# Down projection by seven float32 block products on one core, with block sums on GpSimd and 251-column chunks

## The chip, the cores and the metric

The kernel runs on one core of a Trainium2 chip. Five engines work side by side, each through its own queue in order: TensorE (PE; its weight loads are shown apart as PEld), VectorE (DVE), ScalarE (ACT), GpSimd (POOL) and SyncE (SP), which here only issues DMAs. They wait for each other by semaphores. The metric is the device time of one execution in microseconds (us); three executions of the kernel before have a median of 2159.93 us.

## The reference

```python
x: (8, 3008, 256) float32      w_in: (256, 2048)      w_out: (2048, 256)
X = fft(fft(x, axis=1), axis=2).real        # Fourier mixing of sequence and features
h = X.reshape(24064, 256) @ w_in
g = maximum(0.01 * h, h)                    # leaky ReLU
out = g @ w_out                             # (24064, 256)
```

Everything is in float32, the products on TensorE too.

## The kernel before

**Folding.** The feature transform of width 256 is multiplied into `w_in` once, at the start: `wf` holds the cosine and the sine part (256 rows of 2048 hidden units, two blocks of 128), `wn` the one feature that is its own mirror image. What is left is the sequence transform. The host lays out the rows of x so that a row and its mirror images lie in one tile; `fold_x` (L168) adds and subtracts them, so that a transform needs 3 products of 128 rows for an even and 3 for an odd part.

**Units and blocks.** A unit is one batch b and one parity c of the output frequencies, 16 units in all. `dft` (L276) makes one of a unit's two `mix` tiles (cosine block, sine block): 6 products of 377 or 376 columns into two PSUM tiles, then `butterfly` (L270) copies the even part on ScalarE and makes a plus and a minus half on VectorE. Each half is a block: 32 blocks of 377 or 376 columns. `spread` (L302) fetches the unit's row for the feature that `wn` serves, broadcast to all partitions (`nb`).

**A step** is one block j and one slice f of 128 hidden units: 512 steps.
- `up` (L315): two products of the block's columns, `cos_ps` and `sin_ps` (L320); on VectorE `cos = nb * wn + cos_ps` (L322), then `cos + sin_ps` and `cos - sin_ps` (L325, L326), which are the hidden values of two output columns that mirror each other; on ScalarE the leaky ReLU in place (L327). The result is `g`, five buffers in turn.
- `down` (L330): four products (L337), two column halves of g by two halves of the 256 outputs, added up over the 16 slices in four PSUM banks (`sum_ps`). After the last slice ScalarE copies the four banks (L343) and SP issues two DMAs to the output (L344).

`sum_ps` has four banks, `cos_ps`, `sin_ps` and `dft_ps` share the other four. `down` runs two steps behind `up` (`lag`, L356). The loop (L357) puts `spread`, `fold_x` and `dft` of the next unit beside certain steps, and the load of the next batch's x. The program's scheduler then sets the order on each queue, so that work can stand earlier than the loop says: with two buffers for x the load and the fold of batch 1 stand in the start, among the conversions of the weights (L223 to L229, seven VectorE operations for each 128 x 512 piece, through `raw` tiles of their own, three buffers).

Of the kernel before, what the change touches and what calls it, by code (L numbers as in the profile page):

```python
# [30 lines left out]
F32 = mybir.dt.float32  # L33
I32 = mybir.dt.int32
U32 = mybir.dt.uint32
ALU = mybir.AluOpType
# [5 lines left out]
NI = 3  # L42

KW = [377, 376]
KC = 377
NF = F // P
WN = 512
SLOPE = 0.01
# [60 lines left out]
def chunks():  # L109


    out, at = [], 0
    for b in range(B):
        for c in range(2):
            for sg in range(2):
                out.append((b, c, sg, at, KW[c]))
                at += 2 * KW[c]
    return out, at


def columns():

    at = np.zeros(B * S, np.int64)
    for b, c, sg, first, n in chunks()[0]:
        k = 2 * np.arange(n) + c
        plus, minus = (k, (S - k) % S) if sg == 0 else ((H + k) % S, H - k)
        at[b * S + minus] = first + n + np.arange(n)
        at[b * S + plus] = first + np.arange(n)
    return at
# [3 lines left out]
def tile_fnet_leaky_relu(  # L133
# [55 lines left out]
    wn = const.tile([P, NF], F32, name="wn")  # L189
    wo = const.tile([P, NF, D], F32, name="wo")  # L190
    nyx = const.tile([P, 2, 2, NI, 2, B], F32, name="nyx")
# [59 lines left out]

    def w_out_part(f):
        nf = WN // D
        raw = load_w(w_out[f * P : (f + nf) * P, :].rearrange("(c p) d -> p c d", p=P))
        to_f32(wo[:, f : f + nf, :].rearrange("p c d -> p (c d)"), raw, w_out.dtype)

# [12 lines left out]

    def butterfly(plus, minus, even_ps, odd_ps, m, kw):  # L270
        ev = work.tile([P, KC], F32, tag="ev", bufs=2, name="ev")
        nc.scalar.copy(ev[0:m, 0:kw], even_ps[0:m, 0:kw])  # L272
        nc.vector.tensor_tensor(plus, ev[0:m, 0:kw], odd_ps[0:m, 0:kw], op=ALU.add)  # L273
        nc.vector.tensor_tensor(minus, ev[0:m, 0:kw], odd_ps[0:m, 0:kw], op=ALU.subtract)  # L274

    def dft(u, blk):  # L276

        b, c = u
        z, kw = zs[b], KW[c]
        t = work.tile([P, 2, KC], F32, tag=f"mix{blk}", bufs=2, name=f"mix{blk}")  # L280
# [3 lines left out]
        butterfly(t[:, 0, 0:kw], t[:, 1, 0:kw], pe, po, P, kw)  # L284
        mixed.setdefault(u, {})[blk] = t
# [5 lines left out]
    nc.vector.tensor_tensor(nya[:, 1], nyb[:, 0], nyb[:, 1], op=ALU.subtract)  # L291
    nyq_dram = dram.tile([B, 2, 2, KC], F32, name="nyq_dram")

    def nyquist(c):
        pe, po = dft_ps(), dft_ps()
        for r, pt in ((0, pe), (1, po)):
            sequence(pt, B, lambda i: nya[:, c, i, r, :], r, c)
        t = work.tile([P, 2, KC], F32, tag="mix0", bufs=2, name="nyq")
        butterfly(t[0:B, 0, 0 : KW[c]], t[0:B, 1, 0 : KW[c]], pe, po, B, KW[c])
        nc.sync.dma_start(nyq_dram[:, c, :, 0 : KW[c]], t[0:B, :, 0 : KW[c]])  # L300

    def spread(u):  # L302

        b, c = u
        t = work.tile([P, 2, KC], F32, tag="nb", bufs=2, name="nb")
        nc.sync.dma_start(t[:, :, 0 : KW[c]], nyq_dram[b, c, :, 0 : KW[c]].partition_broadcast(P))
        spreads[u] = t
# [4 lines left out]
    blocks, _ = chunks()  # L312
    steps = [(j, f) for j in range(len(blocks)) for f in range(NF)]

    def up(j, f):  # L315
        b, c, sg, _, n = blocks[j]
        fs = slice(f * P, (f + 1) * P)
        pt = [up_ps("cos_ps"), up_ps("sin_ps")]
        for blk in range(2):
            nc.tensor.matmul(pt[blk][:, 0:n], lhsT=wf[:, blk, fs], rhs=mixed[b, c][blk][:, sg, 0:n], start=True, stop=True)  # L320
        cos = work.tile([P, KC], F32, tag="cos", bufs=3, name="cos")
        nc.vector.scalar_tensor_tensor(cos[:, 0:n], in0=spreads[b, c][:, sg, 0:n], scalar=wn[:, f : f + 1],  # L322
                                       in1=pt[0][:, 0:n], op0=ALU.mult, op1=ALU.add)
        g = work.tile([P, 2, KC], F32, tag="g", bufs=5, name="g")
        nc.vector.tensor_tensor(g[:, 0, 0:n], cos[:, 0:n], pt[1][:, 0:n], op=ALU.add)  # L325
        nc.vector.tensor_tensor(g[:, 1, 0:n], cos[:, 0:n], pt[1][:, 0:n], op=ALU.subtract)  # L326
        nc.scalar.activation(g[:, :, 0:n], g[:, :, 0:n], ACT.Lrelu)  # L327
        hidden[j, f] = g

    def down(j, f):  # L330
        _, _, _, first, n = blocks[j]
        if f == 0:
            sums[j] = [[ps.tile([P, 512], F32, tag="sum", bufs=4, name="sum_ps") for _ in range(2)] for _ in range(2)]
        g = hidden.pop((j, f))
        for h in range(2):
            for i in range(2):
                nc.tensor.matmul(sums[j][h][i][:, 0:n], lhsT=wo[:, f, h * P : (h + 1) * P], rhs=g[:, i, 0:n],  # L337
                                 start=(f == 0), stop=(f == NF - 1))
        if f == NF - 1:
            for h in range(2):  # L340
                o = work.tile([P, 2, KC], F32, tag="o", bufs=2, name="o")
                for i in range(2):
                    nc.scalar.copy(o[:, i, 0:n], sums[j][h][i][:, 0:n])  # L343
                nc.sync.dma_start(out[h * P : (h + 1) * P, first : first + 2 * n].rearrange("p (i n) -> p i n", i=2),  # L344
                                  o[:, :, 0:n])

# [4 lines left out]
    for n in range(4):  # L351
        load_tab(nc.scalar, n, 1)
    for f in range(0, NF, WN // D):
        w_out_part(f)
    nyquist(1)
    lag = 2  # L356
    for at in range(len(steps) + lag):  # L357
        if at < len(steps):
            j, f = steps[at]
            up(j, f)  # L360
            n, sg = divmod(j, 2)
            b, c = units[n]
            if sg == 1 and f == 10 and c == 0 and b + 1 < B:
                load_x(b + 1)
            if n + 1 < len(units):
                if sg == 0 and f == 8:
                    spread(units[n + 1])
                    if c == 1:
                        fold_x(b + 1)
                if sg == 1 and f in (2, 8):  # L370
                    dft(units[n + 1], f // 8)
        if at >= lag:
            down(*steps[at - lag])
# [30 lines left out]
```

## Time and profile before

| | |
|---|---|
| median of three runs | 2159.93 us (2159.39 to 2160.88) |
| profiled execution | 2157.95 us, its span 2155.8 us |
| granted TensorE clock, mean | 0.997 |
| PE busy | 2106.6 us of the span, 6648 instructions |
| VectorE busy | 988.6 us |
| ScalarE busy | 499.9 us |
| GpSimd busy | 1.7 us |
| down products (L337) | 4096 instructions, 1380.2 us busy |
| up products (L320) | 2048 instructions, 815.2 us busy |

A row of grouped instructions reads: line, engine, operation, output<-input (partitions x elements), count, then busy us and mean ns of one, then the engine's idle time just before them and what ended it. A float32 product of the program stands as two MATMUL instructions in the trace. Their ends are modelled and overlap the next one's start, so the spacing of starts, not the length, is the cost. A row of the timeline gives start, length, engine, line and operation, with like instructions merged; in brackets the idle time before it. A row of stretches gives, for each engine or for the named tile's instructions alone, busy time and count.

### The profile page before, as it was taken

What the parts mean: (1) busy time and instruction counts of PE and PEld (TensorE: products, weight loads), DVE (VectorE), ACT (ScalarE), POOL (GpSimd) and SP (SyncE); (2) the same over time, 40 slices, a digit from 0 to 9 for tenths busy, and PEclk for the clock granted to TensorE, in tenths of its full rate; (3) what the DMA queues carried; (4) which work ended last, traced back from release to release, by engine and by line L of the source; (5) the groups of instructions that cost most, each with busy time, mean ns of one, the idle gap of its engine ahead of it and who ended that gap; (6) DMA issues with size and microseconds to landing.
All of it is one profiled execution on the core that took longest, in us unless ns stands there. A gap on an engine that the chain in (4) does not pass through costs nothing.

```text
span 2155.8 us, 17264 instructions
## 1 busy us (share of the span) xinstructions
PE 2106.6 (98%) x6648; PEld 1256.3 (58%) x6648; DVE 988.6 (46%) x1775; ACT 499.9 (23%) x704; POOL 1.7 (0%) x20
## 2 busy tenths in 40 slices
PE   2899999999999999999999999999999999999999
PEld 1455655555555556555655555555655555555565
DVE  6845434454444544436444454445444444444443
ACT  0121222222222221222222222222222222222222
POOL 0000000000000000000000000000000000000000
PEclk9999999999999999999999999999999999999999
DMA  6301000010000200011000100001000000000000
GB/s 263 118 15 59 22 15 22 15 70 10 15 22 15 80 15 2 20 54 42 15 20 2 73 22 15 22 15 62 19 15 22 15 22 1 15 22 15 15 15 15
DMA packets 23962, 70.55 MB, mean 33 GB/s; under 512 B 1968, under 2 KB 12608, under 8 KB 21832
## 3 DMA queue, kind: packets, MB, share of 16 engines
q1 hardware_dynamic: 22728, 64.82, 8.2%
q10 hardware_dynamic: 1152, 4.63, 0.6%
q8 instruction: 52, 0.85, 0.2%
q14 instruction: 30, 0.25, 0.0%
HBM read 44.72 MB, written 24.72 MB: 32 GB/s over the span
## 4 chain that ended last, share of the span: by engine, by line
PE 97%; DVE 1%; DMA 1%; issue 0%; ACTq 0%; ACT 0%; DVEq 0%
PE sum_ps L337 60%; PE sin_ps L320 15%; PE cos_ps L320 15%; PE dft_ps L267 6%; DMA tab<-in_seq_tab_dram 1%; PE up_ps L243 1%; DMA xt<-in_x_dram 1%; PE up_ps L248 0%; DVE win L229 0%; DVE raw L224 0%; DVE xt L173 0%; DVE raw L228 0%; DVE raw L227 0%; DVE raw L226 0%; DVE raw L225 0%
## 5 line engine op out<-in xcount | busy, mean ns | idle before, releaser
L337 PE MATMUL sum_ps<-g,wo 128*128 128x377 f32 (+1 forms) x4096 | 1380.2, 479 | 0.0
L337 PEld LDWEIGHTS sum_ps<-g,wo 128*128 128x128 f32 x4096 | 777.4, 190 | 520.5 <-ACT g L327 0.9
L327 ACT ACTIVATE g<-g 128x752 f32<-128x752 f32 (+1 forms) x512 | 426.0, 832 | 1467.7 <-DVE g L326 1464.7
L322 DVE SCALAR_TENSOR_TENSOR cos<-nb,wn,cos_ps 128x376 f32<-128x376 f32 (+1 forms) x512 | 310.6, 607 | 988.6 <-PE cos_ps L320 988.6
L320 PE MATMUL sin_ps<-mix,wf 128*128 128x376 f32 (+1 forms) x1024 | 408.4, 480 | 4.3 <-DVE g L326 2.8
L320 PE MATMUL cos_ps<-mix,wf 128*128 128x376 f32 (+1 forms) x1024 | 406.8, 478 | 0.0
L325 DVE TENSOR_TENSOR g<-cos,sin_ps 128x376 f32<-128x376 f32 (+1 forms) x512 | 280.4, 548 | 61.9 <-DVE cos L322 1.9
L326 DVE TENSOR_TENSOR g<-cos,sin_ps 128x376 f32<-128x376 f32 (+1 forms) x512 | 277.1, 541 | 0.0
L320 PEld LDWEIGHTS sin_ps<-mix,wf 128*128 128x128 f32 x1024 | 194.1, 190 | 135.1 <-DVE g L326 3.9
L320 PEld LDWEIGHTS cos_ps<-mix,wf 128*128 128x128 f32 x1024 | 192.9, 189 | 131.2 <-issue 0.6
L267 PE MATMUL dft_ps<-tab,xt 128*128 128x377 f32 (+1 forms) x384 | 126.8, 479 | 0.0
L267 PEld LDWEIGHTS dft_ps<-tab,xt 128*128 128x128 f32 x384 | 72.7, 190 | 49.2 <-issue 0.6
L343 ACT COPY o<-sum_ps 128x376 f32<-128x376 f32 (+1 forms) x128 | 53.9, 473 | 77.2 <-PE sum_ps L337 77.2
L243 PE MATMUL up_ps<-win,feat_sb 128*128 128x512 f32 x32 | 23.4, 874 | 40.8 <-DVE win L229 40.8
L273 DVE TENSOR_TENSOR mix<-ev,dft_ps 128x377 f32<-128x377 f32 (+1 forms) x32 | 17.5, 548 | 83.1 <-PE dft_ps L267 80.4
L243 PEld LDWEIGHTS up_ps<-win,feat_sb 128*128 128x128 f32 x32 | 7.5, 261 | 48.0 <-DVE win L229 40.5
L173 DVE TENSOR_TENSOR xt<-xt 128x3072 f32<-128x3072 f32 x8 | 26.8, 3355 | 17.9 <-DMA xt<-in_x_dram 17.9
L272 ACT COPY ev<-dft_ps 128x377 f32<-128x377 f32 (+3 forms) x34 | 15.5, 456 | 15.3 <-PE dft_ps L267 15.3
L274 DVE TENSOR_TENSOR mix<-ev,dft_ps 128x377 f32<-128x377 f32 (+1 forms) x32 | 17.3, 541 | 0.0
L177 DVE TENSOR_TENSOR xt<-xt 128x762 f32<-128x762 f32 x16 | 15.2, 949 | 0.0
L176 DVE TENSOR_TENSOR xt<-xt 128x762 f32<-128x762 f32 x16 | 15.2, 948 | 0.0
L178 ACT COPY xt<-xt 128x6 f32<-128x6 f32 x16 | 2.5, 204 | 50.6 <-DVE xt L173 50.6
(28 smaller groups left out, 128.3 us busy)
## 6 DMA issues: line engine op xcount, KB each, us to landing
xt<-in_x_dram SPq DMA_DIRECT2D x16, 1536.0 KB, 8.3
out_dram<-o SPq DMA_DIRECT2D x32, 377.0 KB, 2.6
out_dram<-o SPq DMA_DIRECT2D x32, 376.0 KB, 2.9
tab<-in_seq_tab_dram ACTq DMA_DIRECT2D x8, 565.5 KB, 14.0
raw<-in_w_in_dram SPq DMA_DIRECT2D x8, 512.0 KB, 3.8
raw<-in_w_out_dram SPq DMA_DIRECT2D x8, 512.0 KB, 3.7
nb<-nyq_dram SPq DMA_DIRECT2D x8, 377.0 KB, 3.3
nb<-nyq_dram SPq DMA_DIRECT2D x8, 376.0 KB, 3.9
```

The costliest lines, as they stand in the source:

```text
L173: nc.vector.tensor_tensor(a, a, z, op=ALU.add)
L243: nc.tensor.matmul(pt, lhsT=feat_sb[:, a, w * P : (w + 1) * P], rhs=win[a], start=(a == 0), stop=(a == 1))
L267: nc.tensor.matmul(ps_t[0:m, 0 : KW[c]], lhsT=z_of(i), rhs=tabs[n, c][:, i, 0 : KW[c]], start=(i == 0), stop=(i == NI - 1))
L273: nc.vector.tensor_tensor(plus, ev[0:m, 0:kw], odd_ps[0:m, 0:kw], op=ALU.add)
L274: nc.vector.tensor_tensor(minus, ev[0:m, 0:kw], odd_ps[0:m, 0:kw], op=ALU.subtract)
L320: nc.tensor.matmul(pt[blk][:, 0:n], lhsT=wf[:, blk, fs], rhs=mixed[b, c][blk][:, sg, 0:n], start=True, stop=True)
L322: nc.vector.scalar_tensor_tensor(cos[:, 0:n], in0=spreads[b, c][:, sg, 0:n], scalar=wn[:, f : f + 1], in1=pt[0][:, 0:n], op0=ALU.mult, op1 ...
L325: nc.vector.tensor_tensor(g[:, 0, 0:n], cos[:, 0:n], pt[1][:, 0:n], op=ALU.add)
L326: nc.vector.tensor_tensor(g[:, 1, 0:n], cos[:, 0:n], pt[1][:, 0:n], op=ALU.subtract)
L327: nc.scalar.activation(g[:, :, 0:n], g[:, :, 0:n], ACT.Lrelu)
L337: nc.tensor.matmul(sums[j][h][i][:, 0:n], lhsT=wo[:, f, h * P : (h + 1) * P], rhs=g[:, i, 0:n], start=(f == 0), stop=(f == NF - 1))
L343: nc.scalar.copy(o[:, i, 0:n], sums[j][h][i][:, 0:n])
```

## The change

The down projection of one step pair is a product of 2 x 2 blocks: the two hidden slices f and f + 8 by the two column halves of g, against the two halves of the outputs. Strassen's scheme, in the form with 7 products and 15 sums, replaces the 8 block products by 7.

- A step now takes two slices, f and `NH + f` (`NH` = 8), and 251 or 250 columns: a unit's 753 or 752 columns are cut in three blocks, so there are 48 blocks of 8 steps, 384 steps. `mix`, `nb` and `nyq_dram` hold a unit's columns in one row.
- `up` makes four products, both slices side by side in one PSUM tile, the second from column n on; L322 becomes two operations of n columns (L352), L325 and L326 one each of 2n (L356, L357), the activation one of 4n (L358).
- Four sums of g's blocks are made on GpSimd (L362 to L365) into a tile `s`, four buffers.
- `down` makes seven products (L380), two to a bank at columns 0 and 256, in the order `turns`. At a block's end one copy on ScalarE (L389) and seven sums on VectorE (L391) give the four output blocks, then two DMAs follow (L393). `lag` is 3.
- The matching sums of `w_out` are made once, on GpSimd, into `wt` (L279), 16 subtractions of 128 x 256.
- x has one buffer in place of two; `raw` takes its buffers from those of `g` (five, shared).

```diff
+UW = [753, 752]
+CW = 251
+NH = NF // 2
...
-        t = xp.tile([P, 2, 2, NI * 2, D], F32, tag="x", bufs=2, name="xt")
+        t = xp.tile([P, 2, 2, NI * 2, D], F32, tag="x", bufs=1, name="xt")
...
-        return work.tile([P, 4, KC], F32, tag="raw", bufs=3, name="raw").rearrange("p f k -> p (f k)")
+        return work.tile([P, 2 * WN], F32, tag="g", bufs=5, name="raw")
...
+        for to, x, y in ((t[0], b[0][1], b[0][0]), (t[1], b[1][1], t[0]), (t[2], b[1][1], b[0][1]), (t[3], b[1][0], t[1])):
+            nc.gpsimd.tensor_tensor(to, x, y, op=ALU.subtract)
...
         for blk in range(2):
-            nc.tensor.matmul(pt[blk][:, 0:n], lhsT=wf[:, blk, fs], rhs=mixed[b, c][blk][:, sg, 0:n], start=True, stop=True)
+            for h in range(2):
+                fs = slice((h * NH + f) * P, (h * NH + f + 1) * P)
+                nc.tensor.matmul(pt[blk][:, h * n : (h + 1) * n], lhsT=wf[:, blk, fs],
+                                 rhs=mixed[b, c][blk][:, at : at + n], start=True, stop=True)
...
+        nc.gpsimd.tensor_tensor(s1, a[1][0], a[1][1], op=ALU.add)
+        nc.gpsimd.tensor_tensor(s2, s1, a[0][0], op=ALU.subtract)
+        nc.gpsimd.tensor_tensor(s3, a[0][0], a[1][0], op=ALU.subtract)
+        nc.gpsimd.tensor_tensor(s4, a[0][1], s2, op=ALU.subtract)
+        hidden[j, f] = a[0][0], a[0][1], s4, a[1][1], s1, s2, s3
+    turns = (0, 1, 5, 6, 4, 2, 3)
...
-        for h in range(2):
-            for i in range(2):
-                nc.tensor.matmul(sums[j][h][i][:, 0:n], lhsT=wo[:, f, h * P : (h + 1) * P], rhs=g[:, i, 0:n],
-                                 start=(f == 0), stop=(f == NF - 1))
+        for i, p in enumerate(turns):
+            nc.tensor.matmul(sums[j][p], lhsT=still[p], rhs=moving[p], start=(f == 0 and i % 2 == 0),
+                             stop=(f == NH - 1), skip_group_check=True)
...
-                    nc.scalar.copy(o[:, i, 0:n], sums[j][h][i][:, 0:n])
+        nc.scalar.copy(q1, p1)
+        for to, x, y in ((c11, q1, p2), (u2, q1, p6), (u3, u2, p7), (v, u2, p5), (c22, u3, p5), (c12, v, p3), (c21, u3, p4)):
+            nc.vector.tensor_tensor(to, x, y, op=ALU.add)
...
-    lag = 2
+    lag = 3
...
-            if sg == 1 and f == 10 and c == 0 and b + 1 < B:
-                load_x(b + 1)
...
+            if c == 0 and part == 2 and f == 6 and b + 1 < B:
+                load_x(b + 1)
```

**One step on TensorE**, in the middle of a block. Before (`mix0`, `mix1` are the unit's two tiles, `wf` and `wo` the weights):

```order
L320 MATMUL cos_ps_723<-mix0_276,wf_74 128x377 [waits DVE_49]
L320 MATMUL sin_ps_724<-mix1_289,wf_74 128x377 [waits DVE_49]
L337 MATMUL sum_ps_687<-g_701,wo_76 128x377 [waits Activation_49]
L337 MATMUL sum_ps_688<-g_701,wo_76 128x377
L337 MATMUL sum_ps_689<-g_701,wo_76 128x377
L337 MATMUL sum_ps_690<-g_701,wo_76 128x377
```

Now (`s` is GpSimd's tile, `wt` the sums of `w_out`):

```order
L347 MATMUL cos_ps_837<-mix0_277,wf_74 128x251 [waits DVE_49]
L347 MATMUL cos_ps_837<-mix0_277,wf_74 128x251
L347 MATMUL sin_ps_838<-mix1_290,wf_74 128x251 [waits DVE_49,PE_49]
L347 MATMUL sin_ps_838<-mix1_290,wf_74 128x251
L380 MATMUL sum_ps_713<-g_771,wo_76 128x251 [waits Activation_49]
L380 MATMUL sum_ps_713<-g_771,wo_76 128x251
L380 MATMUL sum_ps_714<-s_775,wt_77 128x251 [waits Pool_49]
L380 MATMUL sum_ps_714<-s_775,wt_77 128x251
L380 MATMUL sum_ps_715<-s_775,wt_77 128x251
L380 MATMUL sum_ps_715<-s_775,wo_76 128x251 [waits Pool_49]
L380 MATMUL sum_ps_716<-g_771,wt_77 128x251
```

Six products of 377 columns became eleven of 251, two of which wait for GpSimd.

**The end of a block on VectorE.** Before, nothing of it stands there, and one up step follows the other:

```order
L322 SCALAR_TENSOR_TENSOR cos_618<-nb_302,wn_75,cos_ps_614 128x377 [waits PE_49]
L325 TENSOR_TENSOR g_620<-cos_618,sin_ps_615 128x377 [waits DVE_49,PE_49,Activation_49]
L326 TENSOR_TENSOR g_620<-cos_618,sin_ps_615 128x377
L322 SCALAR_TENSOR_TENSOR cos_632<-nb_302,wn_75,cos_ps_628 128x377 [waits PE_49]
L325 TENSOR_TENSOR g_634<-cos_632,sin_ps_629 128x377 [waits DVE_49,PE_49,Activation_49]
```

Now (`e` holds intermediate sums, `o` the output blocks; x2 is two alike rows):

```order
L356 TENSOR_TENSOR g_896<-cos_893,sin_ps_888 128x502 [waits PE_49,DVE_49,Activation_49,Pool_49]
L357 TENSOR_TENSOR g_896<-cos_893,sin_ps_888 128x502
L391 TENSOR_TENSOR o_912<-e_913,sum_ps_713 128x251 [waits Activation_49]
L391 TENSOR_TENSOR e_913<-e_913,sum_ps_714 128x251 [waits PE_49]
L391 TENSOR_TENSOR e_913<-e_913,sum_ps_714 128x251 [waits DVE_49]
L391 TENSOR_TENSOR e_913<-e_913,sum_ps_715 128x251 [waits PE_49]
L391 TENSOR_TENSOR o_912<-e_913,sum_ps_715 128x251 [waits DVE_49] x2
L391 TENSOR_TENSOR o_912<-e_913,sum_ps_716 128x251 [waits PE_49]
L352 SCALAR_TENSOR_TENSOR cos_930<-nb_303,wn_75,cos_ps_924 128x251 [waits PE_49]
```

Seven sums stand between two up steps, in the order in which the banks are filled.

**The fold of batch 1 on VectorE.** Before, it stands in the start, between conversions of `w_in`:

```order
L226 TENSOR_SCALAR raw_111<-raw_111 128x512 [waits DVE_49]
L173 TENSOR_TENSOR xt_816<-xt_816 128x2x1536 [waits DMAHW7_49,DMAHW5_49]
L227 TENSOR_SCALAR raw_111<-raw_111 128x512 [waits DVE_49]
L176 TENSOR_TENSOR xt_816<-xt_816 128x6x127 [waits DVE_49]
L228 SCALAR_TENSOR_TENSOR raw_111<-raw_108,raw_111 128x512 [waits DVE_49]
L177 TENSOR_TENSOR xt_816<-xt_816 128x6x127
```

Now it stands in the loop, in the seventh and eighth step of block 2 and the first ones of block 3:

```order
L356 TENSOR_TENSOR g_1025<-cos_1022,sin_ps_1017 128x502 [waits DVE_49,PE_49,Pool_49]
L357 TENSOR_TENSOR g_1025<-cos_1022,sin_ps_1017 128x502
L189 TENSOR_TENSOR xt_1034<-xt_1034 128x2x1536 [waits DMAHW5_49,DMAHW4_49]
L352 SCALAR_TENSOR_TENSOR cos_1050<-nb_303,wn_75,cos_ps_1044 128x251 [waits PE_49]
L352 SCALAR_TENSOR_TENSOR cos_1050<-nb_303,wn_75,cos_ps_1044 128x251
L192 TENSOR_TENSOR xt_1034<-xt_1034 128x6x127 [waits DVE_49]
L356 TENSOR_TENSOR g_1053<-cos_1050,sin_ps_1045 128x502 [waits DVE_49,PE_49,Pool_49]
L357 TENSOR_TENSOR g_1053<-cos_1050,sin_ps_1045 128x502
L193 TENSOR_TENSOR xt_1034<-xt_1034 128x6x127
```

The fold moved out of the start to the place where its buffer has been read and filled again; the other six folds stand at the like place of their batches.

More of the change, by code (lines that the diff above doesn't have):

```diff
@@ L123, in columns @@
     at = np.zeros(B * S, np.int64)
-    for b, c, sg, first, n in chunks()[0]:
-        k = 2 * np.arange(n) + c
-        plus, minus = (k, (S - k) % S) if sg == 0 else ((H + k) % S, H - k)
+    for b, c, j, n, first in chunks()[0]:
+        col = j + np.arange(n)
+        half = col >= KW[c]
+        k = 2 * np.where(half, col - KW[c], col) + c
+        plus, minus = np.where(half, H + k, k), np.where(half, H - k, (S - k) % S)
         at[b * S + minus] = first + n + np.arange(n)
@@ L339, in down @@
[L339 to L345, printed above, removed]
+            banks = [ps.tile([P, 512], F32, tag="sum", bufs=4, name="sum_ps") for _ in range(4)]
```

97 lines of the change are left out of this document (59 added, 38 removed).

## The prediction

> **What bounds the kernel now.** I read the page's busy shares and its chain first.
>
> ```profile
> span 2155.8 us, 17264 instructions
> PE 2106.6 (98%) x6648; PEld 1256.3 (58%) x6648; DVE 988.6 (46%) x1775; ACT 499.9 (23%) x704; POOL 1.7 (0%) x20
> ...
> PE 97%; DVE 1%; DMA 1%; issue 0%; ACTq 0%; ACT 0%; DVEq 0%
> PE sum_ps L337 60%; PE sin_ps L320 15%; PE cos_ps L320 15%; PE dft_ps L267 6%; DMA tab<-in_seq_tab_dram 1%; PE up_ps L243 1%; DMA xt<-in_x_dram 1%; PE up_ps L248 0%; DVE win L229 0%; DVE raw L224 0%; DVE xt L173 0%; DVE raw L228 0%; DVE raw L227 0%; DVE raw L226 0%; DVE raw L225 0%
> ```
>
> The chain is TensorE's own stream, 60% of it the down products. Busy PE alone proves nothing, so next comes the timeline of PE (start, length): is its stream without gaps, and what does one matmul cost?
>
> ```profile
> 107.46 0.80 PE L320 MATMUL cos_ps<-mix,wf 128*128 128x377 f32 x2
> ...
> 111.26 0.80 PE L320 MATMUL cos_ps<-mix,wf 128*128 128x377 f32 x2
> ...
> 1079.59 0.79 PE L320 MATMUL cos_ps<-mix,wf 128*128 128x376 f32 x2
> 1080.22 0.79 PE L320 MATMUL sin_ps<-mix,wf 128*128 128x376 f32 x2
> 1080.86 2.69 PE L337 MATMUL sum_ps<-g,wo 128*128 128x376 f32 x8
> 1083.38 0.79 PE L320 MATMUL cos_ps<-mix,wf 128*128 128x376 f32 x2
> ...
> 1088.43 3.97 PE L267 MATMUL dft_ps<-tab,xt 128*128 128x377 f32 x12
> ...
> 1092.24 0.48 PE L337 MATMUL sum_ps<-g,wo 128*128 128x376 f32 x1
> ```
>
> Each float32 product stands as two instructions. A step is 12 of them: 3.79 us at 376 columns (3.80 at 377), 316 ns each, evenly. The 512 steps take 256 x 3.80 + 256 x 3.79 = 1943 us. A transform is 12 more, 3.81 us; 30 lie inside the loop, 114 us. What is not PE's steady stream is the start:
>
> ```profile
> 33.37 3.36 DVE L173 TENSOR_TENSOR xt<-xt 128x3072 f32<-128x3072 f32 x1 [1.45 <-DMA xt<-in_x_dram]
> ...
> 94.21 0.53 DVE L326 TENSOR_TENSOR g<-cos,sin_ps 128x377 f32<-128x377 f32 x1
> ...
> 2143.99 7.74 PE L337 MATMUL sum_ps<-g,wo 128*128 128x376 f32 x24
> ```
>
> By 107.46 us PE has issued five up steps and three down steps, 44 instructions or 13.9 us, so the loop counts as begun at 93.5 us. 93.5 + 1943 + 114 = 2151, which is where the last 24 matmuls end; 4.2 us of copies and output follow.
>
> **The change: matmul time.** A step becomes 8 instructions up and 14 down (seven products), all 251 or 250 columns wide, and 384 steps replace 512. Columns up are the same in all; columns down fall to 7/8. What a matmul of 251 costs no row shows; its neighbours are these weight loads, whose starts mark the spacing of full-clock matmuls of 512 columns, and a run of single-column ones:
>
> ```profile
> 52.26 0.19 PEld L243 LDWEIGHTS up_ps<-win,feat_sb 128*128 128x128 f32 x1 [0.24 <-issue]
> 52.69 0.19 PEld L243 LDWEIGHTS up_ps<-win,feat_sb 128*128 128x128 f32 x1 [0.24 <-issue]
> ...
> 53.55 1.62 PE L248 MATMUL up_ps<-feat_sb,win 128*128 128x1 f32 x14
> ```
>
> 512 columns take 430 ns, 376 take 316: 0.84 ns a column. One-column matmuls come about 112 ns apart, which is the weight load alone. So 251 columns give 211 ns, above 112, and the load stays hidden. I take 211.5 ns, as a small fixed cost can't be told from these rows (210.8 without it), and 210.7 at 250. A step is 22 x 211.5 = 4.653 us; 320 x 4.653 + 64 x 4.635 = 1785.6 us. **Minus 157.4 us.** Every nanosecond of error on one matmul is 8.4 us.
>
> ```profile
> L337 PEld LDWEIGHTS sum_ps<-g,wo 128*128 128x128 f32 x4096 | 777.4, 190 | 520.5 <-ACT g L327 0.9 <-issue 0.8
> ```
>
> One load lasts 190 ns but does not lengthen the 316. The Trainium skill, "TensorE: Matmul & The Clock Gate", section "The mechanism", says that weight loads overlap running matmuls only in another row group of the array. The trace disagrees: here all loads use the whole array and are hidden.
>
> **VectorE, ScalarE.** Prices come from rows of the same operations:
>
> ```profile
> L322 DVE SCALAR_TENSOR_TENSOR cos<-nb,wn,cos_ps 128x376 f32<-128x376 f32 x256 | 155.0, 605 | 520.5 <-PE cos_ps L320 520.5
> L325 DVE TENSOR_TENSOR g<-cos,sin_ps 128x376 f32<-128x376 f32 x256 | 139.9, 546 | 32.8 <-DVE cos L322 1.0
> L327 ACT ACTIVATE g<-g 128x752 f32<-128x752 f32 x256 | 212.9, 832 | 736.7 <-DVE g L326 735.2
> L343 ACT COPY o<-sum_ps 128x376 f32<-128x376 f32 x64 | 27.0, 472 | 39.5 <-PE sum_ps L337 39.5
> L244 ACT COPY wf<-up_ps 128x512 f32<-128x512 f32 x8 | 4.7, 585 | 21.9 <-PE up_ps L243 21.9
> L176 DVE TENSOR_TENSOR xt<-xt 128x762 f32<-128x762 f32 x16 | 15.2, 948 | 0.0
> L180 DVE TENSOR_TENSOR xt<-xt 128x1536 f32<-128x1536 f32 x8 | 14.0, 1753 | 0.0
> ```
>
> VectorE's slope is (1753 - 948) / 774 = 1.04 ns an element, ScalarE's copy (585 - 472) / 136 = 0.83. A step's two L352 cost 475 ns each, its two sums of 502 cost 677: 2.3 us of 4.65. The activation of 1004 costs 1.04 us. Both hide.
>
> **Block ends.** One copy and seven chained sums of 416 ns (2.9 us) replace four ScalarE copies, and VectorE's next up step queues behind them. From the start of the last up step before such an end: its VectorE work ends at 3.35 us, the sums at 6.3; the next block's first product comes at 4.65 + 1.69 = 6.34 us, when its bank has been free since the first sum (3.8); the fourth bank is wanted at 8.9. Cost nothing, with 2.5 us of cover.
>
> **GpSimd.** Four sums of 251 a step, then two waits of PE on them. PE wants them about 8 us after the activation, three steps later, so latency is covered; what counts is the rate, 1.16 us each. GpSimd's only rows are tiny:
>
> ```profile
> L179 POOL MEMSET xt<- 128x6 f32 x16 | 1.5, 160 | 1492.9 <-DVE xt L173 1492.9
> ...
> L389 POOL MEMSET const-float32-1.0<- 128x1 f32 x1 | 0.1, 98 | 0.0
> ```
>
> Read as a rate, 62 ns for five more elements (each in another row of the tile) would be 3.2 us at 251, far too slow. VectorE's price for this sum is 0.42 us. I take the end near 0.42, the same operation on the same tiles; up to 2.8 times that is free. The Trainium skill, "GPSIMD Engine Reference", section "Elementwise — side-by-side cycle accounting", has 4497 ns for 2048 elements; my estimate from that is some 0.55 us here plus start-up, and the sum would be the same. No run here shows it.
>
> **The x buffer, one in place of two.** The fold of batch 1 leaves the start, where VectorE is the bound:
>
> ```profile
> 30.00:58.00 28.00, 0.00 (x0) 0.00 (x0) 10.67 (x7) 0.30 (x2) 0.34 (x2) 0.92 0.35 120
> ...
> 16.00:107.00 91.00, 55.41 (x112) 0.92 0.47 165
> ```
>
> The first row is the work on xt in that stretch (third figure: 10.7 us on DVE), the second that on the raw weights (55.4 us for 16 conversions, 3.46 each). Before, the first g ends at 94.7 us, after five conversions of w_out; now g shares its five buffers with raw, and seven come first. 94.7 - 10.7 - 1.45 (its wait for x) + 2 x 3.46 = 89.5; the second g some 3.8 later. The fourth up step waits for that and ends at 95.0, so the loop counts as begun at 95.0 - 4 x 1.69 = 88.2. **Minus 5.3 us**; bounds 0 (something else late) and minus 12.1 (no extra conversions). The subtractions into wt hide on idle GpSimd.
>
> Later x loads are issued only when the last transform has read the buffer; SP's outputs stand ahead of them and have long gone.
>
> ```profile
> DMA to landing us min/median/max: 6.2/8.3/12.9
> ```
>
> The order puts the fold some 10.9 us of PE time after that transform (2.96 + 4.65 + 3.3), against 8.3 + 0.4 for the second load: no wait. The fold's 10.7 us, five steps of 2.3 and seven sums make 25.1 us of VectorE in six steps of 4.65 (27.9). Cost nothing, but with only 2 us of cover at the block end.
>
> **Sum.** 2155.8 - 157.4 - 5.3 = 1993.1 us of span. The profiled execution took 2157.95, 2.15 above its span, and the median is 2.0 above that: **1997 us**.
>
> **Rivals.**
> GpSimd becomes the bound. Beyond 1.16 us a sum, time is 1997 + 1536 x (price - 1.16); from 1.27 us on the kernel is slower than before, at 1.6 us it takes 2670. For: it has no row of such work, and the memset rows allow 3.2. Against: it must be 2.8 times slower than VectorE. Chance 0.11, 0.08 of it slower than before.
>
> VectorE's fold and GpSimd hold each other up. If each of the fold's seven operations waits for one GpSimd sum (0.7 us), VectorE is 5 us later, 3 us beyond the cover, seven times: 2018. For: GpSimd was idle before, so no row shows them together. The Trainium skill, "SBUF — State Buffer", section "Who interferes with whom", has a VectorE instruction with two SBUF inputs and a reading GpSimd one exclude each other; the fold has such inputs, the per-step work does not. Chance 0.10.
>
> Short matmuls cost more than their columns: the 190 ns load leaves 21 ns, and half of the up products write from column 251 of a bank, where before all wide ones start at 0. At 214 ns 2018, at 230 ns 2153. Against: the straight line through 376 and 512. Chance 0.08.
>
> Weight loads in the open, 112 ns on each of 8448: 2943. This is the skill's rule above; it would make today's 316 ns 428. Chance 0.01.
>
> **Chances and range.** 1997 holds with 0.70. Low end: the start's 6.8 us more and 210.8 ns a matmul (6 us), 1984. High end: the fold's 2018 and 3 ns a matmul, 2045. That holds 0.70, 0.10 and about half of the short-matmul case. A run of this kernel can tell about 0.2% (4.3 us). Faster by more: 0.70 + 0.10 + 0.03 + 0.06 = 0.89; within it 0.02; slower 0.09.
>
> **What would show it.** Right: steps of 4.65 us without gaps, about 1.69 of it up; PE still nearly the whole chain; GpSimd rows under 1.16 us; first g near 89 us; no PE wait on L391 sums. Wrong: PE waiting for s at nearly every step, spacing above 214 ns, or PE gaps after each fold.

## The result and the profile after

The changed kernel takes 2001.61 us, median of 4 runs (2000.13 to 2002.70); in the same job the kernel before took 2160.40 us (4 runs, 2159.39 to 2163.11). The ratio is 0.9263, interval 0.9247 to 0.9279: 159 us less, where 163 were forecast. The profiled execution took 2001.1 us, 1.8 above its span, and the median is 0.5 above that.

The head of the page and its chain, after:

```profile
span 1999.3 us, 24452 instructions
PE 1950.6 (98%) x8952; PEld 1691.1 (85%) x8952; DVE 1106.4 (55%) x2111; ACT 439.1 (22%) x496; POOL 1095.0 (55%) x1572
...
PE 96%; DVE 2%; DMA 1%; issue 0%; SPq 0%; DVEq 0%
```

TensorE is the chain as before, GpSimd is busy for half of the span and is not on it. The timeline of PE (start, length) shows the start, the first product behind a block end (134.84), one step in the middle, and the end:

```profile
92.32 2.01 PE L347 MATMUL sin_ps<-mix,wf 128*128 128x251 f32 x4 [3.91 <-DVE g L357]
94.12 1.88 PE L347 MATMUL cos_ps<-mix,wf 128*128 128x251 f32 x4
95.80 1.88 PE L347 MATMUL sin_ps<-mix,wf 128*128 128x251 f32 x4
97.47 1.06 PE L380 MATMUL sum_ps<-g,wo 128*128 128x251 f32 x4
...
100.49 1.01 PE L347 MATMUL cos_ps<-mix,wf 128*128 128x251 f32 x4
...
134.84 1.01 PE L380 MATMUL sum_ps<-g,wo 128*128 128x251 f32 x4
...
1001.28 1.01 PE L347 MATMUL cos_ps<-mix,wf 128*128 128x250 f32 x4
...
1005.94 1.01 PE L347 MATMUL cos_ps<-mix,wf 128*128 128x250 f32 x4
...
1994.23 0.58 PE L380 MATMUL sum_ps<-g,wt 128*128 128x250 f32 x2
```

A step is 4.66 us for 22 instructions, 211.8 ns each; four steps up and one down (46 instructions) lie before the fifth up step at 100.49, so the loop counts as begun at 100.49 - 46 x 0.2118 = 90.75 us. The last matmul ends at 1994.23 + 0.42 = 1994.65, so the steps took 1994.65 - 90.75 - 114.3 (30 transforms) = 1789.6 us, and 4.65 us follow. Against the forecast span of 1993.1 that is +2.55 at the start, +4.0 in the steps and -0.35 behind and in the transforms: +6.2, which is 1999.3. The median is only 4.6 us above the forecast 1997, because it lies 2.3 us above the span here, where the forecast had carried over 4.15 from before; that part is luck.

Stretches of each engine (length; busy time of PE, PEld, DVE, ACT, POOL; granted clock, as a share of full speed; DMA share; GB/s), at the start and in the loop:

```profile
92.00:98.00 6.00, 5.68 (x15) 4.67 (x16) 6.00 (x13) 2.35 (x3) 4.60 (x7) 0.54 0.00 0
130.00:330.00 200.00, 200.00 (x922) 174.18 (x921) 111.28 (x210) 45.06 (x51) 113.16 (x160) 1.00 0.09 33
```

In the loop PE has no gap in 200 us; from 110 us to the end no wait of PE stands in the trace. From 92 to 98 us it ran at a granted clock of 0.54, which is why the up steps above take 1.7 us a half and not 0.85. The new operations, as groups (mean ns after the busy time):

```profile
L352 DVE SCALAR_TENSOR_TENSOR cos<-nb,wn,cos_ps 128x251 f32<-128x251 f32 (+1 forms) x768 | 330.9, 472 | 731.0 <-PE cos_ps L347 731.0
L362 POOL TENSOR_TENSOR s<-g 128x251 f32<-128x251 f32 (+1 forms) x384 | 294.5, 767 | 783.7 <-ACT g L358 783.7
L358 ACT ACTIVATE g<-g 128x1004 f32<-128x1004 f32 (+1 forms) x384 | 399.1, 1039 | 1347.0 <-DVE g L357 1292.3
L364 POOL TENSOR_TENSOR s<-g 128x251 f32<-128x251 f32 (+1 forms) x384 | 253.0, 659 | 0.0
L356 DVE TENSOR_TENSOR g<-cos,sin_ps 128x502 f32<-128x502 f32 (+1 forms) x384 | 260.1, 677 | 50.5 <-DVE cos L352 10.5
```

VectorE's and ScalarE's prices are those forecast (475, 677 and 1040 ns). GpSimd's sum costs 0.66 to 0.77 us in the mean.

### The profile page after: what moved, and what is told of

Its sections match the earlier page's. It is cut to its first block, busy times and chain, and to the rows that moved or that the text cites. A ratio compares the mean times of both kernels' runs of the same rounds, so it can differ in the third digit from the quotient of the medians.

```text
span 1999.3 us, 24452 instructions
## 1 busy us (share of the span) xinstructions
PE 1950.6 (98%) x8952; PEld 1691.1 (85%) x8952; DVE 1106.4 (55%) x2111; ACT 439.1 (22%) x496; POOL 1095.0 (55%) x1572
## 3 DMA queue, kind: packets, MB, share of 16 engines
q8 instruction: 71, 1.16, 0.2%
## 4 chain that ended last, share of the span: by engine, by line
PE 96%; DVE 2%; DMA 1%; issue 0%; SPq 0%; DVEq 0%
PE sum_ps L380 57%; PE sin_ps L347 16%; PE cos_ps L347 16%; PE dft_ps L291 6%; PE up_ps L260 1%; DMA xt<-in_x_dram 1%; PE up_ps L265 0%; DVE raw L240 0%; DVE raw L241 0%; DVE raw L245 0%; DVE raw L244 0%; DVE raw L243 0%; DVE xt L189 0%; DVE win L246 0%; DVE wo L246 0%; DVE raw L242 0%
## 5 line engine op out<-in xcount | busy, mean ns | idle before, releaser
L352 DVE SCALAR_TENSOR_TENSOR cos<-nb,wn,cos_ps 128x251 f32<-128x251 f32 (+1 forms) x768 | 330.9, 472 | 731.0 <-PE cos_ps L347 731.0
L362 POOL TENSOR_TENSOR s<-g 128x251 f32<-128x251 f32 (+1 forms) x384 | 294.5, 767 | 783.7 <-ACT g L358 783.7
L358 ACT ACTIVATE g<-g 128x1004 f32<-128x1004 f32 (+1 forms) x384 | 399.1, 1039 | 1347.0 <-DVE g L357 1292.3
L380 PE MATMUL sum_ps<-s,wt 128*128 128x251 f32 (+1 forms) x2304 | 550.3, 374 | 0.0
L380 PEld LDWEIGHTS sum_ps<-s,wt 128*128 128x128 f32 x2304 | 434.2, 188 | 54.5
L347 PE MATMUL sin_ps<-mix,wf 128*128 128x251 f32 (+1 forms) x1536 | 390.6, 376 | 8.7 <-DVE nyq L300 4.8
L347 PE MATMUL cos_ps<-mix,wf 128*128 128x251 f32 (+1 forms) x1536 | 389.7, 376 | 2.0 <-DVE cos L352 2.0
L380 PE MATMUL sum_ps<-g,wo 128*128 128x251 f32 (+1 forms) x1536 | 388.6, 375 | 0.0
L380 PEld LDWEIGHTS sum_ps<-g,wo 128*128 128x128 f32 x1536 | 291.9, 190 | 40.8
L365 POOL TENSOR_TENSOR s<-g,s 128x251 f32<-128x251 f32 (+1 forms) x384 | 275.1, 716 | 30.1
L356 DVE TENSOR_TENSOR g<-cos,sin_ps 128x502 f32<-128x502 f32 (+1 forms) x384 | 260.1, 677 | 50.5 <-DVE cos L352 10.5
L357 DVE TENSOR_TENSOR g<-cos,sin_ps 128x502 f32<-128x502 f32 (+1 forms) x384 | 257.4, 670 | 0.0
L364 POOL TENSOR_TENSOR s<-g 128x251 f32<-128x251 f32 (+1 forms) x384 | 253.0, 659 | 0.0
L380 PE MATMUL sum_ps<-s,wo 128*128 128x251 f32 (+1 forms) x768 | 225.2, 375 | 0.0
L380 PE MATMUL sum_ps<-g,wt 128*128 128x251 f32 (+1 forms) x768 | 225.2, 375 | 0.0
L380 PEld LDWEIGHTS sum_ps<-s,wo 128*128 128x128 f32 x768 | 145.6, 190 | 17.0
L380 PEld LDWEIGHTS sum_ps<-g,wt 128*128 128x128 f32 x768 | 145.9, 190 | 16.5
```

The source lines that it names most:

```text
L347: nc.tensor.matmul(pt[blk][:, h * n : (h + 1) * n], lhsT=wf[:, blk, fs], rhs=mixed[b, c][blk][:, at : at + n], start=True, stop=True)
L352: nc.vector.scalar_tensor_tensor(cos[:, hs], in0=spreads[b, c][:, at : at + n], scalar=wn[:, h * NH + f : h * NH + f + 1], in1=pt[0][:, hs ...
L356: nc.vector.tensor_tensor(g[:, 0], cos[:, 0 : 2 * n], pt[1][:, 0 : 2 * n], op=ALU.add)
L357: nc.vector.tensor_tensor(g[:, 1], cos[:, 0 : 2 * n], pt[1][:, 0 : 2 * n], op=ALU.subtract)
L358: nc.scalar.activation(g, g, ACT.Lrelu)
L362: nc.gpsimd.tensor_tensor(s1, a[1][0], a[1][1], op=ALU.add)
```

## The experiments

Each is the changed kernel with one edit, if nothing else is said. Five ask where the 159 us come from, one asks what the three-step lag covers, six ask what bounds the start.

**Eight products (e_eight).** Same chunks, same up steps; the down step is the plain one, with no GpSimd sums, one bank for each result and four ScalarE copies at a block's end.

```diff
-        nc.gpsimd.tensor_tensor(s1, a[1][0], a[1][1], op=ALU.add)
...
-        for i, p in enumerate(turns):
-            nc.tensor.matmul(sums[j][p], lhsT=still[p], rhs=moving[p], start=(f == 0 and i % 2 == 0),
...
+        for d in range(2):
+            for r in range(2):
+                for h in range(2):
+                    nc.tensor.matmul(sums[j][d][r], lhsT=wo[:, h, f, d * P : (d + 1) * P], rhs=moving[r][h],
...
+                nc.scalar.copy(o[:, d, r * n : (r + 1) * n], sums[j][d][r])
```

> Tiling, chunks, lag and start as in the changed kernel, but the plain eight block products of each step in place of Strassen's seven, no block sums on GpSimd, and four ScalarE copies at a block's end. Theory (the gain is the seventh-for-eighth product alone, each instruction 0.212 us of PE): 384 steps x 2 instructions x 0.212 = 163 us more than the changed kernel's 2002, so 2164, level with the kernel before. Rival (the gain came from the chunking, the start or the longer lag): well under 2100.

Measured: 2166.87 us, ratio 1.0031 (1.0019 to 1.0044). Its timeline of PE:

```profile
1003.41 1.01 PE L347 MATMUL cos_ps<-mix,wf 128*128 128x251 f32 x4
...
1005.11 3.57 PE L374 MATMUL sum_ps<-g,wo 128*128 128x251 f32 x16
1008.51 1.01 PE L347 MATMUL cos_ps<-mix,wf 128*128 128x251 f32 x4
```

A step is 5.10 us for 24 instructions against 4.66 for 22. The gain is the product that is left out: 165 us lie between the two kernels, where two instructions of 0.212 us in each of 384 steps make 163. The chunks, the start, the lag and the x buffer, which both have, come to 0.3% more than before.

**GpSimd twice (e_pool_twice).** Every one of the four sums is issued two times, the second writing the same values (s1 is shown, s2, s3 and s4 likewise).

```diff
         nc.gpsimd.tensor_tensor(s1, a[1][0], a[1][1], op=ALU.add)
+        nc.gpsimd.tensor_tensor(s1, a[1][0], a[1][1], op=ALU.add)
...
```

> The changed kernel with each of GpSimd's four block sums per step issued twice (the second writes the same values again). Theory (GpSimd is hidden only as long as its step fits into PE's 4.66 us): eight sums of 0.67 to 0.73 us make 5.4 to 5.8 us, GpSimd becomes the bound, 384 x 5.4 to 5.8 + some 100 us of start and end = 2170 to 2330. Rival (the sums overlap each other, so that GpSimd has a hidden reserve): 2002 as before.

Measured: 2298.87 us, ratio 1.0645 (1.0623 to 1.0666). From its page, and the first product with s in two steps that follow each other on PE:

```profile
PE 2105.9 (92%) x8952; PEld 1675.9 (73%) x8952; DVE 1115.9 (49%) x2111; ACT 439.2 (19%) x496; POOL 2117.8 (92%) x3108
...
POOL 75%; PE 19%; issue 3%; DVE 2%; DMA 1%; POOLq 0%; ACT 0%; SPq 0%; DVEq 0%
```

```profile
1003.73 1.54 PE L384 MATMUL sum_ps<-s,wt 128*128 128x251 f32 x6 [0.32 <-POOL s L365]
...
1009.32 1.54 PE L384 MATMUL sum_ps<-s,wt 128*128 128x251 f32 x6 [0.32 <-POOL s L365]
```

Now the chain is GpSimd's, and TensorE waits for s. A step takes 5.59 us for eight sums, 0.70 each: this is the rate without pauses. So four sums fill 2.8 of 4.66 us, and GpSimd would have become the bound at 1.66 times its price.

**The sums on VectorE (e_vector_sums).** All four of them.

```diff
-        nc.gpsimd.tensor_tensor(s1, a[1][0], a[1][1], op=ALU.add)
+        nc.vector.tensor_tensor(s1, a[1][0], a[1][1], op=ALU.add)
...
```

> The changed kernel with the four block sums of each step on VectorE. Theory: a step on VectorE is 2.24 us of its own work, four sums at 0.42, a share of the block end 0.32, of fold and transforms 0.30: 4.55 of PE's 4.66 us. It fits on the mean, but the fold and the block ends leave no room, so PE waits there: 2010 to 2060. Rival (VectorE can take it all without loss, GpSimd wasn't needed): 2002. Rival (the in-order queue makes VectorE wait for ScalarE at every step): 2200 or more.

Measured: 2011.76 us, ratio 0.9315 (0.9301 to 0.9329). Its waits from 110 us on:

```profile
PEld sum_ps L380 <- DVE o L391: 10.9, 22, 1.2
...
PE sum_ps L380 <- DVE o L391: 4.4, 8, 0.8
```

VectorE is busy for 80% of the time from there on and late only at block ends, where its seven sums stand behind more work. So GpSimd is worth 10 us of the 159: the scheme pays even without it.

**189 and 126 columns (e_188, e_126).** Four and six chunks for three; where the loop over parts asks for it, the two transforms stay in the second and third part. The diff is that of 189; for 126 there stand 126 and 6.

```diff
-CW = 251
+CW = 189
...
-            n, part = divmod(j, 3)
+            n, part = divmod(j, 4)
...
-                else:
+                elif part < 3:
                     dft(units[n + 1], part - 1)
```

> The changed kernel with four chunks of 189 or 185 columns per unit in place of three of 251, so 64 blocks and 512 steps. Theory (a matmul costs 0.833 ns a column plus some 2.7 ns, and a weight load is hidden until its 112 ns spacing binds): 159.5 ns each, 512 x 22 x 159.5 = 1797 us against 1790 now, so about 2009. Rival (the 190 ns that one weight load lasts is a floor): 190 ns each, 2140 us of steps, 2350 in all.

> The changed kernel with six chunks of 126 columns or fewer per unit in place of three of 251, so 96 blocks and 768 steps. Theory (columns or the weight load, whichever is longer, set the spacing): the line gives 107.5 ns, the weight load's own spacing is 112, so 112 ns, 768 x 22 x 112 = 1892 us of steps, about 2100, unless VectorE or GpSimd takes over: GpSimd's step is then 4 x 0.45 = 1.8 us of PE's 2.46 and VectorE's 1.8. Rival (the 190 ns that one load lasts becomes a floor here): 3210 us of steps. Rival (the load is hidden at any width): 1816 us of steps, about 2025.

Measured: 2008.64 us, ratio 0.9301 (0.9282 to 0.932), and 2098.86 us, ratio 0.9713 (0.9695 to 0.9731). The timelines of PE, first with 189, then with 126 columns:

```profile
1006.75 0.80 PE L347 MATMUL cos_ps<-mix,wf 128*128 128x189 f32 x4
...
1010.27 0.80 PE L347 MATMUL cos_ps<-mix,wf 128*128 128x189 f32 x4
```

```profile
1002.93 0.61 PE L347 MATMUL cos_ps<-mix,wf 128*128 128x126 f32 x4
...
1005.39 0.61 PE L347 MATMUL cos_ps<-mix,wf 128*128 128x126 f32 x4
```

3.52 and 2.46 us for 22 instructions: 160.0 and 111.8 ns. With the 316 at 376 columns and the 211.8 at 251, the first three lie on one line of 0.83 ns a column and some 3 ns besides; at 126 the line would give 108, and what is measured is the 112 ns at which weight loads followed one another in the kernel before; no wait of PE stands in that trace from 110 us on. By these spacings the weight load begins to bind between 126 and 189 columns. 251 has room.

**A lag of one step (e_lag1).**

```diff
-    lag = 3
+    lag = 1
```

> The changed kernel with down one step behind up in place of three. Theory (from the start of an up step, g is ready at 4.5 us, GpSimd's third sum at 6.6 and its fourth at 7.2; with a lag of one PE wants them at 6.3, 7.2 and 8.5): the plain steps still fit, and PE waits only where VectorE is late, some 3 us at each of the seven folds and under 1 us at block ends: 2010 to 2060. Rival (GpSimd's latency needs the long lag): a wait of 1 us or more at each of 384 steps, 2400 or more.

Measured: 2039.22 us, ratio 0.9437 (0.942 to 0.9455). Its timeline of PE behind the first fold of x that lies in the loop, which begins at 204.75 us:

```profile
210.69 1.54 PE L380 MATMUL sum_ps<-s,wt 128*128 128x251 f32 x6 [1.80 <-POOL s L363]
```

The waits for s from 110 us on, the lines of the matmuls and of the weight loads (total us, times, longest):

```profile
PEld sum_ps L380 <- POOL s L363: 36.4, 29, 3.1
PE sum_ps L380 <- POOL s L363: 25.0, 27, 2.7
```

The same work in the same amount, with PE asking for the sums two steps earlier, costs 38 us; waits for s are two thirds of that by TensorE's rows and nearly all of it by those of its weight loads. All but the last of them, at the end of the kernel, stand behind the seven folds in the loop. So in a plain step one step of lag covers GpSimd's latency, and it is for the folds that more is needed.

**The kernel before with one x buffer (e_before_x1).**

```diff
-        t = xp.tile([P, 2, 2, NI * 2, D], F32, tag="x", bufs=2, name="xt")
+        t = xp.tile([P, 2, 2, NI * 2, D], F32, tag="x", bufs=1, name="xt")
```

> The kernel before with one x buffer in place of two, nothing else. Theory (the start is bound by VectorE, and the fold of batch 1 leaves it): 10.7 us of fold and 1.45 us of waiting for x go, 2160 - 12 = 2148. Rival (the start is bound by PE or by the loads): 2160. Rival (the later loads come too late with one buffer): above 2160.

Measured: 2146.81 us, ratio 0.9937 (0.9925 to 0.995). The timeline of ACT:

```profile
84.25 0.83 ACT L327 ACTIVATE g<-g 128x754 f32<-128x754 f32 x1 [8.22 <-DVE g L326]
```

The first activation starts 10.5 us earlier than before (94.78): the fold of batch 1 was in the way there, and taking it out of the start is worth 0.6% by itself. The changed kernel got only 2.75 us of that.

**Own buffers for the raw weights (e_raw_own).**

```diff
-        return work.tile([P, 2 * WN], F32, tag="g", bufs=5, name="raw")
+        return work.tile([P, 2 * WN], F32, tag="raw", bufs=3, name="raw")
```

> The changed kernel with the raw weight tiles in three buffers of their own again, not in those of g. Theory (the first g waits for seven conversions of w_out because of the shared buffers, for five without): the loop starts 2 x 3.46 us of VectorE work earlier, 2002 - 7 = 1995. Rival (the start is bound by something else, so that the order of the conversions costs nothing): 2002.

Measured: 1999.48 us, ratio 0.9254 (0.9241 to 0.9266). The activations, of the changed kernel and then of this one:

```profile
92.21 1.04 ACT L358 ACTIVATE g<-g 128x1004 f32<-128x1004 f32 x1 [17.40 <-DVE g L357]
95.31 1.04 ACT L358 ACTIVATE g<-g 128x1004 f32<-128x1004 f32 x1 [2.06 <-DVE g L357]
```

```profile
86.27 1.04 ACT L358 ACTIVATE g<-g 128x1004 f32<-128x1004 f32 x1 [10.46 <-DVE g L357]
94.11 1.04 ACT L358 ACTIVATE g<-g 128x1004 f32<-128x1004 f32 x1 [6.80 <-DVE g L357]
```

A miss, and a useful one: 2.1 us less than the changed kernel where 7 were expected, and the intervals of the two ratios overlap. The first g comes 5.9 us earlier, the second only 1.2: VectorE still does all eight conversions of w_out, some of them now between the two. TensorE's longest wait behind the first g is this one of e_raw_own:

```profile
94.12 0.69 PE L380 MATMUL sum_ps<-s,wo 128*128 128x251 f32 x2 [1.64 <-POOL s L365]
```

It waits for the last sum of the first step. In this trace three subtractions into wt stand ahead of that sum on GpSimd, from 89.98 to 92.88 us, beside conversions on VectorE. So what counts is not which buffer g waits for but how much weight work VectorE and GpSimd have to do before TensorE can run on.

**The conversions beside the first steps (e_wout_late, e_wout_halves).** Both have the own buffers; in the first, three of the four parts of w_out are converted behind the up steps 1, 3 and 5, in the second one half part at a time behind six steps.

```diff
-    for f in range(0, NH, WN // D):
-        w_out_part(f)
+    w_out_part(0)
...
             up(j, f)
+            if at in (1, 3, 5):
+                w_out_part(at + 1)
```

> The changed kernel with raw in three buffers of its own, and all but the first quarter of the w_out conversions issued beside the loop's steps 1, 3 and 5, just ahead of the down steps that need them. Theory (VectorE bounds the start, and its slack in the loop, about half of each step, can take conversions): the first g no longer waits for more than three conversions, the loop counts as begun some 9 us earlier, 1993. Rival (what is taken out of the start comes back as PE waits in the first steps): 1998 to 2002.

> As the kernel with the late w_out conversions, but one conversion per step, in steps 1, 2, 3, 4, 6 and 7, in place of two at once in steps 1, 3 and 5. Theory (two conversions at once held back a g in that run, and PE waited 3.5 us for it once): that wait goes, 1991 - 3.5 = 1987. Rival (VectorE's total in the first steps is what counts, not how it is spread): 1991.

Measured: 1990.88 us, ratio 0.9215 (0.9202 to 0.9227), and 1991.89 us, ratio 0.9217 (0.9205 to 0.923). Both are faster than the kernel before and the changed kernel; the second misses the 1987 us expected of it and is no faster than the first. The first activation and a row of PE of e_wout_late, and a row of PE of e_wout_halves:

```profile
78.95 1.04 ACT L358 ACTIVATE g<-g 128x1004 f32<-128x1004 f32 x1 [4.46 <-DVE g L357]
```

```profile
108.31 1.09 PE L347 MATMUL sin_ps<-mix,wf 128*128 128x251 f32 x4 [3.49 <-DVE g L357]
```

```profile
115.24 0.69 PE L382 MATMUL sum_ps<-g,wo 128*128 128x251 f32 x2 [3.04 <-DVE wo L246]
```

The first g is 13.3 us earlier than in the changed kernel, and 10.1 us of span stay; part of the rest comes back at 108, where a step takes 10.07 us in place of 4.66: a wait of 3.5 us and slower matmuls behind it (granted clock 0.72 from 108 to 114 us). Spreading the conversions more finely took this wait away and put one of 3.0 on wo in its place. By these two rows the first steps are short of VectorE time, however it is ordered.

**The subtractions into wt out of the way (e_wt_late, e_wt_held).** The prediction had these 16 GpSimd operations free. In the trace of after the conversions of w_out are longer than before: the timelines of DVE and of POOL over the same two microseconds:

```profile
68.25 0.41 DVE L243 TENSOR_SCALAR raw<-raw 128x512 int32<-128x512 int32 x1
68.65 0.88 DVE L240 TENSOR_SCALAR raw<-raw 128x512 int32<-128x512 int32 x1
69.45 0.95 DVE L244 TENSOR_SCALAR raw<-raw 128x512 int32<-128x512 int32 x1
```

```profile
68.23 1.00 POOL L279 TENSOR_TENSOR wt<-wo 128x256 f32<-128x256 f32 x1
69.21 0.91 POOL L279 TENSOR_TENSOR wt<-wo,wt 128x256 f32<-128x256 f32 x1
```

The first of these conversion rows keeps its 0.41 us, and the subtraction that begins with it takes 1.00, where the one before it in the trace took 0.73. The next two take 0.88 and 0.95 us; rows of the same kind and size with no subtraction beside them take 0.41. So each of the two engines holds the other up. The first kernel issues 12 of the 16 later in the program's text; the second holds them there as well, by a small ScalarE copy into wt that they have to overwrite. The diff is that of the second; without the lines on seed it is the first. wt_part holds the subtractions that stood in w_out_part, and the first four stay where they were.

```diff
             up(j, f)
+            if at in (1, 2, 3):
+                seed = hidden[j, f][0][:, 0:8].rearrange("p (i c w) -> p i c w", i=4, c=2)
+                nc.scalar.copy(wt[:, :, 2 * at : 2 * at + 2, 0:1], seed)
+                wt_part(2 * at)
```

> The changed kernel with 12 of the 16 GpSimd subtractions that fill wt issued behind the up steps 1, 2 and 3 instead of beside the conversions of w_out. In the changed kernel's trace the one-input conversion rows (the TENSOR_SCALAR lines) take 0.42 us alone and 0.88 to 0.95 us where such a subtraction runs beside them; over the start the sixteen conversions cost 3.98 us each where they cost 3.73 before the change, 3.95 us in all, nearly all of it ahead of the first g. Theory: VectorE and GpSimd hold each other up there, and this is why the first g ended at 92.2 us and not at the forecast 89.5. Then with the subtractions away the conversions are back at 3.73 to 3.80 each, the first activation starts 2 to 3 us earlier (89.5 to 90.3 us), and the kernel gains 1 to 2.5 us: about 1999.5 us. Rival: the conversions are slowed by something else (transfers that write beside them, the matrix unit reading): then they stay at 3.98, the first activation stays at 92.2 and the time at 2001.6.

> The changed kernel with 12 of the 16 GpSimd subtractions into wt really held back: three small ScalarE copies from the activation's output into wt stand ahead of them, behind the up steps 1, 2 and 3, so that they can't be issued beside the conversions of w_out (all values are written over by the subtractions). Theory as for the run before: the excess of the conversions (3.98 us each where 3.73 stood before the change) is GpSimd's company; with it away the L240 rows are back from 545 to some 430 ns in the mean, the first activation starts 2 to 3 us earlier, 89.2 to 90.2 us, and the kernel gains 1 to 2.5 us, about 1999.5 us. GpSimd's own backlog is the risk: five steps' sums of 2.85 us and 12 subtractions of 0.7 us make 22.6 us from 91 us on, done at 114, where TensorE wants the fifth step's sums at 115; a wait of a microsecond at the fourth or fifth down step would eat half of the gain. Rival: transfers or TensorE slow the conversions: then L240 stays at 545 ns and the first activation at 92.2 us.

Measured for e_wt_late: 2000.87 us, ratio 0.9264 (0.9251 to 0.9276), no difference, and it says nothing on the question: the scheduler put the subtractions back to where their inputs are ready, and GpSimd's order is that of the changed kernel. Measured for e_wt_held: 1997.56 us, ratio 0.925 (0.9238 to 0.9263), a span of 1996.3, 3.0 us less. The two intervals overlap, but the slowest of its five executions, 1999.82, is faster than the fastest of the changed kernel, 2000.13. One conversion row by its shape in the start, of the changed kernel and of e_wt_held, and e_wt_held's first activation:

```profile
L240 DVE TENSOR_SCALAR raw<-raw 128x512 int32<-128x512 int32 x16 | 8.7, 546 | 0.0
```

```profile
L240 DVE TENSOR_SCALAR raw<-raw 128x512 int32<-128x512 int32 x16 | 7.1, 442 | 0.0
```

```profile
89.60 1.04 ACT L361 ACTIVATE g<-g 128x1004 f32<-128x1004 f32 x1 [14.85 <-DVE g L360]
```

The first activation starts at 89.60, where the changed kernel has 92.21. Summed over its seven lines a conversion takes 3.98 us in the changed kernel, 3.81 here and 3.73 before the change. These rows overlap a little, so the work on raw is better read as VectorE's busy time (the figure behind the length of the stretch; before the change 55.41), again of the changed kernel and of e_wt_held:

```profile
16.00:107.00 91.00, 57.74 (x112) 0.89 0.38 130
```

```profile
16.00:107.00 91.00, 55.07 (x112) 0.91 0.38 131
```

The subtractions cost VectorE 2.3 us, and holding twelve of them back returns 2.7. The share of the DMA engines is 0.38 in both, so the amount of transfers, the rival, isn't what differs.

## Why the prediction was right, and where it was off

**The mechanism: right.** TensorE's columns set the time, and one product in eight of the down step goes. e_eight, which puts it back, shows it.

**The matmul's price: right to 0.2%.** 211.8 ns for 211.5 (210.7 at 250). Over 8448 instructions this is 1789.6 us for 1785.6, the +4.0 us above: the fixed part of some 3 ns that the rows of before could not tell from none. The Trainium skill, "TensorE: Matmul & The Clock Gate", section "The mechanism", says in its list of what overlaps that a weight load runs beside a matmul only in another row group; its text above that list also names a background weight buffer. The runs disagree with the list: in e_188 a matmul's whole period is 160 ns, less than the 190 ns that one full-array weight load lasts.

**GpSimd: right in outcome, not in price.** The price taken was near 0.42 us; measured are 0.66 to 0.77 in the mean and 0.70 in a row, over one and a half times as much. It stayed under 1.16, the room that the prediction had named, and by e_pool_twice the wall stands where the forecast put it: eight sums in a step of 4.65 are 0.58 us each, and 0.70 is above that.

**VectorE, ScalarE, block ends, x loads: right.** At the first block end the timeline of DVE reads:

```profile
131.72 0.41 DVE L391 TENSOR_TENSOR o<-e,sum_ps 128x251 f32<-128x251 f32 x1
...
133.25 1.06 DVE L391 TENSOR_TENSOR o<-e,sum_ps 128x251 f32<-128x251 f32 x3
```

The sums are done at 134.3, and PE's next products into these banks begin at 134.84 without a wait. The x loads land in 6.5 us in the median (14.5 for one), and no fold keeps PE waiting, though VectorE idles for 0.61 us before the first of them in the loop until its load has landed.

**The fold against GpSimd: the rival's lock is there, its price is not.** DVE and POOL at the first fold in the loop:

```profile
195.96 3.36 DVE L189 TENSOR_TENSOR xt<-xt 128x3072 f32<-128x3072 f32 x1 [0.61 <-DMA xt<-in_x_dram]
196.59 3.30 POOL L362 TENSOR_TENSOR s<-g 128x251 f32<-128x251 f32 x1 [1.90 <-ACT g L358]
...
199.86 0.62 POOL L364 TENSOR_TENSOR s<-g 128x251 f32<-128x251 f32 x1
```

A sum of the size that takes 0.62 us a moment later takes 3.30 here, and ends 0.57 us after the fold's first operation does. This is what the Trainium skill, "SBUF — State Buffer", section "Who interferes with whom", calls an exclusive lock, and the trace agrees. With three steps of lag nothing reaches TensorE; with one step it does (e_lag1, the 1.80 us wait). The rival needed VectorE to be the late one, by 5 us a fold with 2 us of cover. VectorE's seven operations of a fold did grow, from 10.7 to 11.7 us in the mean of the eight, which is inside the cover; most of the waiting was GpSimd's, and the lag covers that.

**The start: the step that failed.** Minus 5.3 us was forecast, minus 2.75 came. "The subtractions into wt hide on idle GpSimd" was wrong. They slow VectorE's conversions beside them, and VectorE is the bound there: 2.3 us more of its time than before the change. Hold twelve of the sixteen back and the first activation starts at 89.60, close to the forecast 89.5, and the span is 3.0 us less. The same section of the Trainium skill, "SBUF — State Buffer", "Who interferes with whom", lists `tensor_scalar`, here the TENSOR_SCALAR rows, among the VectorE operations that can take the port pair shared with GpSimd; it gives conditions, and no run here shows whether they hold. The prediction read that section for the fold and not for the start.

A second thing stands beside it: TensorE, idle before, ran the last half of the third up step and the fourth up step at a granted clock of 0.54. From 92.32 to 97.47 three half steps took 5.15 us where full clock needs 2.54. At full clock the last half would have begun when the second g came, at 95.28, and ended at 96.1; so about 1.3 of the 2.55 us are the clock's, by this reckoning, and the rest VectorE's. VectorE's delay alone is larger, 2.0 us at the second g (95.28 for 93.3). But the forecast had the whole fourth up step wait for that g, where only its last half does, and this hid 0.85 us. The two may not be separate causes: in e_wt_held, where TensorE had been idle for 3.09 us and not 3.91, the three half steps took 4.76 us. What sets the clock was not tried.

That the first g waits for seven conversions by its buffer, which the forecast used, is so (e_raw_own moves it by 5.9 us). But the start didn't follow the first g alone: in e_raw_own TensorE then waited for a sum of GpSimd that stood behind subtractions.

## What to carry to other kernels

A scheme that trades a product for sums pays as long as the sums of a step take their engine less time than the step takes, and the lag to the consumer is longer than their longest hold-up: price the rate and the lag apart. Work put on an idle engine is free only if it does not hold up the engine that is the bound at that time, so look for each stretch at who shares what. Where a start is bound by one engine, count all of the work that it must do before the stream can run on, not what stands before the first result; moving a part of it into the steady loop (e_wout_late) gained 10.7 us more here, 2.1 of them with the own raw buffers alone.

## What the hardware showed beyond that

- VectorE's one-input 512-element operation went from 0.41 to as much as 0.95 us beside a GpSimd subtraction, while its two-input rows with one input in PSUM kept their price (L356: 677 ns with GpSimd busy for 55% of the time, as priced from a kernel in which it was idle).
- A GpSimd sum of some 0.6 to 0.7 us took 3.30 us beside one VectorE operation of 3.36 us with both inputs in SBUF and ended 0.57 us after it: held, not slowed in proportion.
- The spacing of float32 matmuls followed the columns down to 160 ns at 189 and stood at the load's 112 ns at 126.
